# A decode kernel bound by its loads: TensorE's program in eleven rounds, another split of wo, and fifteen small unused transfers on SyncE's queue

## The chip, the cores and the metric

The kernel runs on one core of a Trainium2 chip. The metric is device time in microseconds (us) of one execution, the median of several; lower is better. Three runs of the kernel before took 675.99, 676.03 and 676.4 us. A profile is one further execution, recorded by the hardware; its span goes from the first to the last recorded instruction.

## The reference

One decode step for two sequences (B = 2, D = 448): a cached attention with 16 heads of 256, 4096 keys and values each, a small dense block with ReLU, and a gate that mixes the two.

```python
g = sigmoid((x * gate_w).sum(-1, keepdims=True))
q = (x @ wq).reshape(B, 1, H, Dh)                      # H = 16, Dh = 256
p = softmax(einsum("bhqd,bhkd->bhqk", q, k_cache) * Dh ** -0.5)
a = einsum("bhqk,bhkd->bhqd", p, v_cache).reshape(B, 1, H * Dh) @ wo
b = maximum(x @ w1, 0) @ w2                            # w1: 448 x 1792, w2: 1792 x 448
return g * a + (1 - g) * b
```

All arrays are float32. The caches alone are 2 x 134 MB.

## The kernel before, in words

The work is cut into U = 32 units, one per head and sequence. A unit is one array `kv[u]` of 128 rows of 16384 numbers (8.4 MB): 8192 of keys, 8192 of values. SBUF holds three units, `slot[0]` to `slot[2]`, and everything that is loaded goes through these slots.

**SyncE (SP)** issues every transfer, in program order, on one queue. At the start it issues `wq` into slot 0 (together with x and the gate's weights) and units 0 and 1 into slots 1 and 2. Then, unit by unit, it waits until VectorE has freed a slot (`freed`) and issues the load of the unit three further on (L166, L169). The last unit comes in two halves, keys (L171) and values (L172). Behind it, as slots come free, SP issues `w1` and `w2` of the dense block into slot 0 (L174, L175) and `wo` into slot 1 (L179). `wo` is 32 chunks of 448 columns, 0.23 MB each, and goes out in parts: the parts of `ACC`, of 14 and 9 chunks, then those of `DIRECT`, of 4, 2, 2 and 1. Each part has its own semaphore. Last, SP waits for the result (`res_ok`) and stores it (L182).

**TensorE (PE)** first does the gate (L196) and the two halves of the projection of q (L207), whose contraction of 448 is three chunks of 128 rows and one of 64. A written matmul call of float32 stands in the trace as two LDWEIGHTS and two MATMUL. Each unit's scores are 16 calls (L121, in `unit_pe`). Ten rounds of a loop do three units each, and the last two units stand behind the loop, written out. Then comes the tail: the hidden layer (L234, in `hidden`), small transposes and sums for the softmax over the four groups of keys (L241, L245, L251), the hidden layer's transposes (L256, L258), its second product (L264) and `wo`. The chunks of `ACC` are added to `acc`, on top of the second product, one call of 448 columns a chunk (L276), four column groups in turn. VectorE copies `acc` to `a_sb` (L368), four calls fold it into `z` (L284), and the chunks of `DIRECT` go straight into `z`, four calls of 112 columns a chunk (L289).

**VectorE (DVE)** takes for each unit the maximum of the scores (L135) and, after ScalarE's exponentials (L128), eight multiply-and-sum passes over the values (L141); the last one raises `freed`. It also spreads x into `xr` at the start (L336) and copies `z` to `res` at the end (L370).

The order of all this is written by hand: each engine's instructions run in the order of the text and wait on semaphores.

Of the kernel before, what the change touches and what calls it, by code (L numbers as in the profile page):

```python
# [19 lines left out]
def gated_mix_decode(nc, wq, kv, wm, wo, out):  # L20
    U, _, SW = kv.shape
    D = 448
    B = 2
    RB = R // B
    T, DH = 2, 256
# [18 lines left out]
    def ev():  # L44
        sems.append(nc.alloc_semaphore(f"e{len(sems)}"))
        return sems[-1]
# [13 lines left out]

    out_sem = nc.alloc_semaphore("out_sem")
    slot_in = [ev() for _ in range(SLOTS)]
    last_v, w1_in, w2_in = ev(), ev(), ev()
    wo_in = [ev() for _ in ACC + DIRECT]
    scored, maxed, raised, queried, freed = (ev() for _ in range(5))

# [5 lines left out]
    sel = sb("sel", P, R)  # L72
    par = sb("par", P, B)
    fold = sb("fold", P, RB, B)
    xr = sb("xr", P, KC, P // B, B)
    ge = sb("ge", P, 1)
    gp = sb("gp", P, 1)
    omg = sb("omg", P, 1)
# [6 lines left out]
    p = sb("p", P, SG)  # L85
# [10 lines left out]
    pa = ps("pa", P, CW)  # L96
# [2 lines left out]
    acc = ps("acc", P, CW)  # L99
    z = ps("z", P, CW)  # L100

    def rows_of(c, i=0):
        return slice(0, P) if c < KF else slice(i * HP, (i + 1) * HP)

    def x_of(r, c, n=R):
        return xr[r, c].rearrange("p r b -> p (r b)")[:, :n]

    xg = slot[0][:, NW:wq.shape[1]].rearrange("p (c b) -> p c b", c=KC)

    ident_0, ident_ok, par_ok = ev(), ev(), ev()  # L110
# [34 lines left out]
    LOOP = (U - 2) // SLOTS  # L145
    U1 = LOOP * SLOTS
# [8 lines left out]
    with nc.Block(no_gpsimd_drain=True) as block:  # L155

        @block.sync
        def _(_e):
            sp.wait_ge(q_mm, 2)
            sp.dma_start(slot[0], kv[2]).then_inc(slot_in[0], 16)  # L160
            with nc.Fori(0, LOOP - 1, engines=(ET.SP,)) as r:
# [12 lines left out]
            sp.dma_start(w1, wm[:, :W1]).then_inc(w1_in, 16)  # L174
            sp.dma_start(w2, wm[:, W1:]).then_inc(w2_in, 16)  # L175
            sp.wait_ge(freed, U - 1)
            k = 0
            for n, s in zip(ACC + DIRECT, wo_in):
                sp.dma_start(w_o[:, k * D:(k + n) * D], wo[:, k * D:(k + n) * D]).then_inc(s, 16)  # L179
                k += n  # L180
            sp.wait_ge(res_ok, 1)
            sp.dma_start(out, res[0:7 * 15 + 1:7, :]).then_inc(out_sem, 16)  # L182

        @block.gpsimd
        def _(_e):
            pool.memset(ident, 0.0).then_inc(ident_0, 1)
            pool.wait_ge(ident_0, 1)
# [3 lines left out]
        @block.tensor  # L191
        def _(_e):
            pe.wait_ge(x_ok, 1)
            for c in range(KC):
                r = rows_of(c)
                m = pe.matmul(pa[:, :1], x_of(r, c, P), xg[r, c, B:], start=(c == 0), stop=(c == KC - 1))  # L196
            m.then_inc(gate_mm, 1)
            W = 2 * KF * DH
            for i in range(2):
                w = slot[0][:, i * NW // 2:(i + 1) * NW // 2]  # L200
                if i:
                    pe.wait_ge(q_ok, i)
                for c in range(KC):
                    for g in range(G):
                        r = rows_of(c, g // 2)
                        at = g * W + c * CW if c < KF else G * W + g % 2 * CW
                        m = pe.matmul(pb[g * R:(g + 1) * R, :], x_of(r, c), w[r, at:at + CW], start=(c == 0),  # L207
                                      stop=(c == KC - 1))
                m.then_inc(q_mm, 1)
                pe.wait_ge(q_ok, i + 1)  # L210
                if i:
                    pe.wait_ge(qt_ok, i)
                else:
                    pe.wait_ge(ident_ok, 1)
                for k in range(2 * T):
                    m = pe.transpose(pc[:, k * P:(k + 1) * P], q[:, k * P:(k + 1) * P], ident)
                m.then_inc(q_tr, 1)
            with nc.Fori(0, LOOP, 1, engines=(ET.PE,)) as r:
                for k in range(SLOTS):
                    s = (k + 1) % SLOTS  # L220
                    unit_pe(k, r * SLOTS + (k + 1), r * 16 + (32 if s == 0 else 16), s)
            for k in range(U - U1):
                s = (k + 1) % SLOTS
                unit_pe(k, U1 + k + 1, LOOP * 16 + 16, s)

            half = W1 // 2

            def hidden(lo, hi):
                for c in range(lo, hi):
                    for g in range(G):  # L230
                        j, i = divmod(g, 2)
                        at = i * half + (j * KF + c if c < KF else 2 * KF) * FG
                        r = rows_of(c, j)
                        m = pe.matmul(pa[g * R:(g + 1) * R, :FG], x_of(r, c), w1[r, at:at + FG], start=(c == 0),  # L234
                                      stop=(c == KC - 1))
                return m
# [6 lines left out]
            hidden(2, 3)  # L243
# [3 lines left out]
            hidden(3, 4).then_inc(hid_mm, 1)  # L247
            pe.wait_ge(os_ok, 1)
            n = HH * B * J
            for g in range(G):  # L250
# [27 lines left out]
                    k += 1  # L278
            m.then_inc(acc_mm, 1)
            for i, a in enumerate(DIRECT):  # L280
                if i == FOLD_AT:
                    pe.wait_ge(a_ok, 1)
                    for g in range(G):
                        pe.matmul(z[g * R:(g + 1) * R, :DG], fold.rearrange("p r b -> p (r b)"),  # L284
                                  a_sb[:, g * DG:(g + 1) * DG], start=(i == 0), stop=False)
                pe.wait_ge(wo_in[len(ACC) + i], 16)
                for _ in range(a):
                    for g in range(G):
                        m = pe.matmul(z[g * R:(g + 1) * R, :DG], o_of(k),  # L289
                                      w_o[:, k * D + g * DG:k * D + (g + 1) * DG], start=(k == n and FOLD_AT > 0),  # L290
                                      stop=(k == NO - 1))
                    k += 1
            m.then_inc(z_mm, 1)

        @block.scalar
        def _(_e):
# [11 lines left out]
            with nc.Fori(0, LOOP, engines=(ET.Activation,)) as r:  # L308
# [20 lines left out]
        def _(_e):  # L329
# [6 lines left out]
            dve.tensor_copy(xr, xg[:, :, None, :B].to_broadcast([P, KC, P // B, B])).then_inc(x_ok, 1)  # L336
# [6 lines left out]
            with nc.Fori(0, LOOP, engines=(ET.DVE,)) as r:  # L343
# [87 lines left out]
```

## Time and profile before

| what | value |
|---|---|
| median of three runs | 676.03 us |
| the profiled execution's own time | 675.96 us |
| its span | 674.4 us |
| busy, share of the span | PE 32%, DVE 50%, ACT 7% |
| loaded | 289.5 MB, 429 GB/s over the span |
| instructions recorded | 3971 |

The shares of busy time are means over the whole span. Loads run through the whole of it, in the order in which SP issued them, and a transfer is spread over 16 DMA engines. A row of the timeline reads: start, duration, engine, line, operation, tiles, count, and in brackets how long the engine was idle before it and what ended that. In a row of the stretches (windows), the last two columns are the mean busy share of the 16 DMA engines and the GB/s moved.

### The profile page before, as it was taken

To read this page: it belongs to the slowest core of one execution; us is meant where nothing else is said; L and a number is where in the kernel's file an instruction comes from. 1 tells how busy PE (TensorE), PEld (TensorE's weight loads), DVE (VectorE), ACT (ScalarE), POOL (GpSimd) and SP (SyncE) were. 2 spreads that over 40 slices of the span, in tenths; PEclk is the share of its full clock that TensorE was granted. 3 is DMA by queue.
4 is the path that set the end of the run, shared out by engine and by line. 5 is a ranking of instruction groups with operands and counts; after the bars stand their busy time and mean duration, and the time that the engine had idled before them with its cause. 6 is when DMAs were issued, how large, how long until landed. Compare 5 with 4: busy or idle time off the path is not lost.

```text
span 674.4 us, 3971 instructions
## 1 busy us (share of the span) xinstructions
PE 218.0 (32%) x1309; PEld 53.4 (8%) x1309; DVE 340.4 (50%) x563; ACT 46.3 (7%) x107; POOL 0.7 (0%) x6
## 2 busy tenths in 40 slices
PE   0733221333332123333322233333222333332445
PEld 0200000000000000000000000000000000000012
DVE  0024566545455665544656654455666445456760
ACT  0010000000000000000000000000000000000110
POOL 0000000000000000000000000000000000000000
PEclk9975667767655666766666676665567667655869
DMA  9999999999999999999999999999999999999997
GB/s 381 428 436 435 436 435 435 435 435 435 435 435 435 435 435 435 435 435 435 431 435 435 435 435 435 435 435 435 435 431 435 435 435 435 435 435 408 423 439 303
DMA packets 6084, 289.61 MB, mean 429 GB/s; under 512 B 704, under 2 KB 832, under 8 KB 1216
## 3 DMA queue, kind: packets, MB, share of 16 engines
q1 hardware_dynamic: 6080, 289.55, 99.3%
q8 instruction: 3, 0.05, 0.0%
q14 instruction: 1, 0.01, 0.0%
HBM read 289.54 MB, written 0.01 MB: 429 GB/s over the span
## 4 chain that ended last, share of the span: by engine, by line
DMA 70%; DVE 13%; PE 10%; issue 6%; ACT 1%; DVEq 1%; SPq 0%; ACTq 0%
DMA slot<-in_kv 65%; DVE slot L141 11%; PE sc L121 9%; DMA slot<-in_wo 4%; DVE nm L135 2%; ACT p L128 1%; DVEq L141 1%; PE acc L276 0%; PE z L289 0%; SPq L166 0%; DVE a_sb L368 0%; DVEq L135 0%; ACTq L128 0%; PE z L284 0%; SPq L67 0%
## 5 line engine op out<-in xcount | busy, mean ns | idle before, releaser
L121 PE MATMUL sc<-slot,qc 128*32 128x512 f32 x1024 | 187.2, 898 | 413.1 <-DMA slot<-in_kv 413.1
L141 DVE SCALAR_TENSOR_TENSOR slot<-slot,p 128x1024 f32<-128x1024 f32 x256 | 295.9, 1222 | 47.2 <-ACT p L128 45.8
L135 DVE TENSOR_REDUCE nm<-sc 128x1024 f32 (+1 forms) x32 | 39.2, 1225 | 243.4 <-PE sc L121 243.4
L121 PEld LDWEIGHTS sc<-slot,qc 128*32 128x32 f32 x1024 | 42.0, 156 | 557.6 <-issue 538.6
L128 ACT ACTIVATE p<-sc,nm 128x1024 f32<-128x1024 f32 x32 | 35.6, 1113 | 563.2 <-DVE nm L135 563.2
L141 DVE DVE_READ_ACCUMULATOR slot<-slot,p (+1 forms) x256 | 21.3, 83 | 0.0
L207 PE MATMUL pb<-slot,xr 128*32 128x512 f32 (+1 forms) x64 | 9.5, 732 | 0.0
L336 DVE COPY xr<-slot 128x512 f32<-128x512 f32 x1 | 0.4, 426 | 17.9 <-DMA slot<-in_wq 17.9
L234 PE MATMUL pa<-slot,xr 128*32 128x448 f32 (+1 forms) x32 | 5.2, 761 | 12.3 <-DMA slot<-in_wm 12.3
L196 PE MATMUL pa<-slot,xr 128*128 128x1 f32 (+1 forms) x8 | 2.0, 357 | 20.7 <-DVE xr L336 20.7
L368 DVE COPY a_sb<-acc 128x448 f32<-128x448 f32 x1 | 0.6, 625 | 14.0 <-PE acc L276 14.0
L276 PE MATMUL acc<-slot,oc 128*32 128x448 f32 x46 | 5.6, 542 | 4.2 <-DMA slot<-in_wo 4.2
L128 ACT ACTIVATION_READ_ACCUMULATOR p<-sc,nm (+1 forms) x32 | 6.2, 193 | 0.0
L130 ACT ACTIVATE qc<-qt 128x2 f32 (+1 forms) x31 | 5.9, 192 | 0.0
L264 PE MATMUL acc<-slot,hr 128*32 128x448 f32 x28 | 3.2, 541 | 1.0 <-ACT hr L323 1.0
L196 PEld LDWEIGHTS pa<-slot,xr 128*128 128x128 f32 (+1 forms) x8 | 1.9, 322 | 20.7 <-DVE xr L336 20.7
L207 PEld LDWEIGHTS pb<-slot,xr 128*32 128x32 f32 (+1 forms) x64 | 2.0, 129 | 5.9 <-issue 5.9
L276 PEld LDWEIGHTS acc<-slot,oc 128*32 128x32 f32 x46 | 1.7, 109 | 8.1 <-issue 5.8
L234 PEld LDWEIGHTS pa<-slot,xr 128*32 128x32 f32 (+1 forms) x32 | 0.9, 140 | 14.8 <-DMA slot<-in_wm 13.2
L289 PE MATMUL z<-slot,oc 128*32 128x112 f32 x72 | 1.9, 259 | 0.0
L301 ACT ACTIVATE q<-pb 128x512 f32<-128x512 f32 x2 | 1.2, 597 | 9.1 <-PE pb L207 9.1
L364 DVE COPY oc<-pc 128x256 f32<-128x256 f32 x4 | 1.4, 418 | 0.7 <-PE pc L251 0.7
(45 smaller groups left out, 16.9 us busy)
## 6 DMA issues: line engine op xcount, KB each, us to landing
slot<-in_kv SPq DMA_DIRECT2D x2, 4096.0 KB, 34.9
slot<-in_wq SPq DMA_DIRECT2D x1, 7174.0 KB, 19.4
slot<-in_wm SPq DMA_DIRECT2D x2, 3136.0 KB, 31.2
slot<-in_wo SPq DMA_DIRECT2D x1, 3136.0 KB, 24.6
slot<-in_wo SPq DMA_DIRECT2D x1, 2016.0 KB, 29.0
slot<-in_wo SPq DMA_DIRECT2D x1, 896.0 KB, 30.7
slot<-in_wo SPq DMA_DIRECT2D x2, 448.0 KB, 31.6
slot<-in_kv SPq DMA_DIRECT2D x31, 39.7
```

The lines of the kernel that those rows point to most:

```text
L121: m = pe.matmul(sc[g * R:(g + 1) * R, c * CW:(c + 1) * CW], qc[:, s, t:t + 1].to_broadcast([P, R]), slot[s][:, lo:lo + CW], start=(t == 0) ...
L128: act.activation(p, sc, AF.Exp, bias=nm[:, bass.ds(u, 1)], accum_out=ls[:, bass.ds(u, 1)]).then_inc(raised, 1)
L130: act.activation(qc[:, s_next, :], qt[:, bass.ds(u + 1, 1), :].rearrange("p o t -> p (o t)"), AF.Copy).then_inc(queried, 1)
L135: dve.tensor_reduce(nm[:, bass.ds(u, 1)], sc, axis=AX.X, op=ALU.max, negate=True).then_inc(maxed, 1)
L141: m = dve.scalar_tensor_tensor(v, v, 1.0, p, op0=ALU.mult, op1=ALU.mult, accum_out=ov[:, bass.ds(u, 1), j].rearrange("p o -> p o"))
L196: m = pe.matmul(pa[:, :1], x_of(r, c, P), xg[r, c, B:], start=(c == 0), stop=(c == KC - 1))
L207: m = pe.matmul(pb[g * R:(g + 1) * R, :], x_of(r, c), w[r, at:at + CW], start=(c == 0), stop=(c == KC - 1))
L234: m = pe.matmul(pa[g * R:(g + 1) * R, :FG], x_of(r, c), w1[r, at:at + FG], start=(c == 0), stop=(c == KC - 1))
L264: pe.matmul(acc[g * R:(g + 1) * R, :D], hr[:, k, :], w2[:, k * D:(k + 1) * D], start=(k < G), stop=False)
L276: m = pe.matmul(acc[g * R:(g + 1) * R, :D], o_of(k), w_o[:, k * D:(k + 1) * D], start=False, stop=(k >= n - G))
L289: m = pe.matmul(z[g * R:(g + 1) * R, :DG], o_of(k), w_o[:, k * D + g * DG:k * D + (g + 1) * DG], start=(k == n and FOLD_AT > 0), stop=(k = ...
L364: m = dve.tensor_copy(oc[:, h], pc[:, h * B * J:(h + 1) * B * J].rearrange("p (o b j) -> p j o b", o=1, b=B) .to_broadcast([P, J, RB, B]))
```

## The change

It has four parts.

1. **TensorE's program gets shorter.** All 32 units run in one loop of eleven rounds. A round does units 0 and 1 of three, then asks whether it is the last, and does the third unit only if not. The other engines' loops keep their ten rounds and the two units behind them.
2. **The last 64 rows of the contraction are done for two groups at once.** A new tile `xl` (128 x 64, cleared by GpSimd, filled by two copies of VectorE) holds x for both halves of the rows, with zeros elsewhere, so that two calls of 128 rows and 64 columns take the place of four calls of 64 rows and 32 columns. `xn` holds x for the gate's last chunk. A function `project` does this for the projection of q and for the hidden layer; the arrays are laid out on the host to match.
3. **`wo` goes out in other parts**: 14, 8 and 4 chunks into `acc`, then 3, 2 and 1 straight into `z`. There are six transfers, as before.
4. **Fifteen small transfers** stand behind `wo` on SP's queue. SP waits until all 32 units are freed, then reads n rows of 256 + 16 n columns of `wo`, for n from 15 down to 1, into slot 2, which nobody reads any more. At its end, behind the store of the result, SP waits until they have landed.

```diff
-ACC = (14, 9)
-DIRECT = (4, 2, 2, 1)
-FOLD_AT = 0
+ACC = (14, 8, 4)
+DIRECT = (3, 2, 1)
...
+    def project(dst, w, at, at_last, n, lo, hi):
+        for c in range(lo, min(hi, KF)):
+            for g in range(G):
+                m = pe.matmul(dst[g * R:(g + 1) * R, :n], x_of(c), w[:, at(c, g):at(c, g) + n], start=(c == 0), stop=False)
+        if hi == KC:
+            for i in range(2):
+                m = pe.matmul(dst[i * HP:(i + 1) * HP, :n], xl.rearrange("p j r b -> p (j r b)"),
+                              w[:, at_last(i):at_last(i) + n], start=False, stop=True)
+        return m
...
             for n, s in zip(ACC + DIRECT, wo_in):
                 sp.dma_start(w_o[:, k * D:(k + n) * D], wo[:, k * D:(k + n) * D]).then_inc(s, 16)
                 k += n
+            sp.wait_ge(freed, U)
+            for n in range(15, 0, -1):
+                w = 256 + 16 * n
+                sp.dma_start(slot[2][:n, n * CW:n * CW + w], wo[:n, :w]).then_inc(small_in, 16)
             sp.wait_ge(res_ok, 1)
             sp.dma_start(out, res[0:7 * 15 + 1:7, :]).then_inc(out_sem, 16)
+            sp.wait_ge(small_in, 16 * 15)
...
-            with nc.Fori(0, LOOP, 1, engines=(ET.PE,)) as r:
-                for k in range(SLOTS):
-                    s = (k + 1) % SLOTS
-                    unit_pe(k, r * SLOTS + (k + 1), r * 16 + (32 if s == 0 else 16), s)
-            for k in range(U - U1):
-                s = (k + 1) % SLOTS
-                unit_pe(k, U1 + k + 1, LOOP * 16 + 16, s)
+            with nc.Fori(0, LOOP, engines=(ET.PE,)) as r:
+                u0 = pe.snap(r * SLOTS)
+                def units(lo, hi):
+                    for k in range(lo, hi):
+                        unit_pe(k, u0 + (k + 1), r * 16 + (32 if k == SLOTS - 1 else 16), (k + 1) % SLOTS)
+                units(0, FULL)
+                with pe.If_lt(pe.to_reg(r), LOOP - 1):
+                    units(FULL, SLOTS)
+                pe.end_ifs()
...
             dve.wait_ge(slot_in[0], 16)
-            dve.tensor_copy(xr, xg[:, :, None, :B].to_broadcast([P, KC, P // B, B])).then_inc(x_ok, 1)
+            dve.tensor_copy(xr, xg[:, :KF, None, :B].to_broadcast([P, KF, P // B, B]))
+            dve.tensor_copy(xn, xg[:, KF:, :B].to_broadcast([P, P // B, B]))
+            dve.wait_ge(xl_0, 1)
+            for j in range(2):
+                m = dve.tensor_copy(xl[j * HP:(j + 1) * HP, j], xg[j * HP:(j + 1) * HP, KF:, :B]
+                                    .to_broadcast([HP, RB, B]))
+            m.then_inc(x_ok, 1)
```

The built programs show what moves. On TensorE, from the loop of the units to the hidden layer, the rows before are these (`sc` are the scores, `qc` the unit's q, `pa` the hidden layer):

```order
L121 MATMUL sc<-slot_50,qc 32x512 x16
L116 REGISTER_ALU
L121 MATMUL sc<-slot_51,qc 32x512 x16
L115 REGISTER_ALU
L116 REGISTER_ALU
L121 MATMUL sc<-slot_49,qc 32x512 x16
L218 REGISTER_ALU
L218 COMPARE_AND_BRANCH
L121 MATMUL sc<-slot_50,qc 32x512 x16
L121 MATMUL sc<-slot_51,qc 32x512 x16
L234 MATMUL pa<-slot_49,xr 32x448 x8
```

At the same place of the changed program stand these:

```order
L129 MATMUL sc<-slot_50,qc 32x512 x16
L124 REGISTER_ALU
L129 MATMUL sc<-slot_51,qc 32x512 x16
L236 COMPARE_AND_BRANCH
L123 REGISTER_ALU
L124 REGISTER_ALU
L129 MATMUL sc<-slot_49,qc 32x512 x16
L236 UNCONDITIONAL_BRANCH
L228 REGISTER_ALU
L228 COMPARE_AND_BRANCH
L109 MATMUL pa<-slot_49,xr 32x448 x8
```

The two written-out units behind the loop are gone, 32 calls, and a branch stands ahead of the third unit. With the other parts, TensorE's program goes from 229 written matmul calls to 182.

On SP, from `wo` on, the rows before are these:

```order
L179 DMA slot_50<-in_wo 128x6272
L179 DMA slot_50<-in_wo 128x4032
L179 DMA slot_50<-in_wo 128x1792
L179 DMA slot_50<-in_wo 128x896 x2
L179 DMA slot_50<-in_wo 128x448
L182 DMA out<-res 16x112
```

In the changed program `wo` (L189) is cut otherwise, and the small transfers (L194), of which the first six are shown, stand between it and the store:

```order
L189 DMA slot_50<-in_wo 128x6272
L189 DMA slot_50<-in_wo 128x3584
L189 DMA slot_50<-in_wo 128x1792
L189 DMA slot_50<-in_wo 128x1344
L189 DMA slot_50<-in_wo 128x896
L189 DMA slot_50<-in_wo 128x448
L194 DMA slot_51<-in_wo 15x496
L194 DMA slot_51<-in_wo 14x480
L194 DMA slot_51<-in_wo 13x464
L194 DMA slot_51<-in_wo 12x448
L194 DMA slot_51<-in_wo 11x432
L194 DMA slot_51<-in_wo 10x416
```

The store of the result is now sixteenth behind the last part of `wo` on this queue instead of first.

More of the change, by code (lines that the diff above doesn't have):

```diff
@@ L62, in gated_mix_decode @@
     slot_in = [ev() for _ in range(SLOTS)]
-    last_v, w1_in, w2_in = ev(), ev(), ev()
+    last_v, w1_in, w2_in, small_in = (ev() for _ in range(4))
     wo_in = [ev() for _ in ACC + DIRECT]
@@ L100, in gated_mix_decode, with x_of @@
     z = ps("z", P, CW)
[L102 to L106, printed above, removed]
+    def x_of(c, n=R):
+        return xr[:, c].rearrange("p r b -> p (r b)")[:, :n]
+    def project(dst, w, at, at_last, n, lo, hi):
[7 more added lines that the diff above has]
+        return m
     xg = slot[0][:, NW:wq.shape[1]].rearrange("p (c b) -> p c b", c=KC)
-    ident_0, ident_ok, par_ok = ev(), ev(), ev()
+    ident_0, ident_ok, par_ok, xl_0 = ev(), ev(), ev(), ev()
     x_ok, gate_mm, gate_ok, ge_ok, gp_ok, omg_ok = (ev() for _ in range(6))
@@ L160, in _ @@
             sp.dma_start(slot[0], kv[2]).then_inc(slot_in[0], 16)
-            with nc.Fori(0, LOOP - 1, engines=(ET.SP,)) as r:
+            with nc.Fori(0, LOOP - 2, engines=(ET.SP,)) as r:
                 u0 = sp.snap(r * SLOTS)
@@ L189, in _, with pe_main @@
                                channel_multiplier=1).then_inc(ident_ok, 1)
-        @block.tensor
-        def _(_e):
+        def pe_main():
             pe.wait_ge(x_ok, 1)
             for c in range(KC):
-                r = rows_of(c)
-                m = pe.matmul(pa[:, :1], x_of(r, c, P), xg[r, c, B:], start=(c == 0), stop=(c == KC - 1))
+                r = slice(0, P if c < KF else HP)
+                m = pe.matmul(pa[:, :1], x_of(c, P) if c < KF else xn[r].rearrange("p r b -> p (r b)"), xg[r, c, B:],
+                              start=(c == 0), stop=(c == KC - 1))
             m.then_inc(gate_mm, 1)
@@ L199, in _ @@
             for i in range(2):
-                w = slot[0][:, i * NW // 2:(i + 1) * NW // 2]
                 if i:
                     pe.wait_ge(q_ok, i)
[L203 to L209, printed above, removed]
+                project(pb, slot[0][:, i * NW // 2:(i + 1) * NW // 2], lambda c, g: g * W + c * CW,
+                        lambda i: G * W + i * CW, CW, 0, KC).then_inc(q_mm, 1)
                 pe.wait_ge(q_ok, i + 1)
@@ L217, in _, with pe_tail @@
                 m.then_inc(q_tr, 1)
-            with nc.Fori(0, LOOP, 1, engines=(ET.PE,)) as r:
-                for k in range(SLOTS):
-                    s = (k + 1) % SLOTS
-                    unit_pe(k, r * SLOTS + (k + 1), r * 16 + (32 if s == 0 else 16), s)
-            for k in range(U - U1):
-                s = (k + 1) % SLOTS
-                unit_pe(k, U1 + k + 1, LOOP * 16 + 16, s)
+            with nc.Fori(0, LOOP, engines=(ET.PE,)) as r:
[7 more added lines that the diff above has]
+                pe.end_ifs()
+        def pe_tail():
             half = W1 // 2
             def hidden(lo, hi):
[L229 to L236, printed above, removed]
+                return project(pa, w1, lambda c, g: g // 2 * half + (g % 2 * KF + c) * FG,
+                               lambda i: i * half + 2 * KF * FG, FG, lo, hi)
             pe.wait_ge(w1_in, 16)
@@ L242, in _ @@
             pe.transpose(pc[:U, P:2 * P], ls, ident).then_inc(ml_tr, 1)
-            hidden(2, 3)
+            hidden(2, KF)
             pe.wait_ge(wb_ok, 1)
@@ L246, in _ @@
                       stop=True).then_inc(wp_mm, 1)
-            hidden(3, 4).then_inc(hid_mm, 1)
+            hidden(KF, KC).then_inc(hid_mm, 1)
             pe.wait_ge(os_ok, 1)
@@ L289, in _ @@
                         m = pe.matmul(z[g * R:(g + 1) * R, :DG], o_of(k),
-                                      w_o[:, k * D + g * DG:k * D + (g + 1) * DG], start=(k == n and FOLD_AT > 0),
+                                      w_o[:, k * D + g * DG:k * D + (g + 1) * DG], start=False,
                                       stop=(k == NO - 1))
@@ L293, in _ @@
             m.then_inc(z_mm, 1)
+        @block.tensor
+        def _(_e):
+            pe_main()
+            pe_tail()
         @block.scalar
@@ L307, in _ @@
             act.activation(qc[:, 1, :], qt[:, 0, :], AF.Copy).then_inc(queried, 1)
-            with nc.Fori(0, LOOP, engines=(ET.Activation,)) as r:
+            with nc.Fori(0, LOOP - 1, engines=(ET.Activation,)) as r:
                 u0 = act.snap(r * SLOTS)
@@ L342, in _ @@
             dve.tensor_scalar(omg, gp, -1.0, 1.0, op0=ALU.mult, op1=ALU.add).then_inc(omg_ok, 1)
-            with nc.Fori(0, LOOP, engines=(ET.DVE,)) as r:
+            with nc.Fori(0, LOOP - 1, engines=(ET.DVE,)) as r:
                 u0 = dve.snap(r * SLOTS)
@@ L405 @@
     full = full.reshape(P, KF, 2, G, 2 * DH).transpose(2, 0, 3, 1, 4).reshape(2, P, -1)
-    last = last.reshape(HP, 2, 2, 2, 2 * DH).transpose(1, 2, 0, 3, 4).reshape(2, P, -1)
+    last = last.reshape(HP, 2, 2, 2, 2 * DH).transpose(1, 3, 0, 2, 4).reshape(2, P, -1)
     wq = np.concatenate([full, last], 2)
@@ L410 @@
     full, last = blocks(B_w1)
-    full = full.reshape(P, KF, 2, 2, FG).transpose(0, 3, 2, 1, 4).reshape(P, 2, -1)
-    last = last.reshape(HP, 2, 2, FG).transpose(1, 0, 2, 3).reshape(P, 2, FG)
+    full = full.reshape(P, KF, 2, 2, FG).transpose(0, 2, 3, 1, 4).reshape(P, 2, -1)
+    last = last.reshape(HP, 2, 2, FG).transpose(2, 0, 1, 3).reshape(P, 2, FG)
     w1 = np.concatenate([full, last], 2).reshape(P, -1)
```

12 lines of the change are left out of this document (8 added, 4 removed).

## The prediction

> **What bounds the kernel now.** I read the chain that ended last first, then the GB/s by slice, then the end of the chain in order of time, and last the stretches of the final microseconds. From the page:
>
> ```profile
> GB/s 381 428 436 435 436 435 435 435 435 435 435 435 435 435 435 435 435 435 435 431 435 435 435 435 435 435 435 435 435 431 435 435 435 435 435 435 408 423 439 303
> ...
> DMA 70%; DVE 13%; PE 10%; issue 6%; ACT 1%; DVEq 1%; SPq 0%; ACTq 0%
> ...
> L121 PE MATMUL sc<-slot,qc 128*32 128x512 f32 x1024 | 187.2, 898 | 413.1 <-DMA slot<-in_kv 413.1
> ```
>
> The loads move 435 GB/s in nearly every slice, so no engine holds them up for long. TensorE's scores are busy for 187.2 us and idle for 413.1 us before them, every time until a load: 12.9 us a unit (413.1 / 32). What a microsecond of engine work is worth is decided only behind the last load. The chain there, from the window 600 to 676 us (start, us, what):
>
> ```profile
> 637.47 0.33 SPq L179
> ...
> 637.84 29.02 DMA slot<-in_wo
> ...
> 666.90 2.46 PE acc L276 x18
> ...
> 669.38 0.64 DVE a_sb L368
> ...
> 670.06 0.40 PE z L284 x8
> ...
> 670.46 1.77 PE z L289 x72
> ...
> 672.25 0.28 DVE res L370
> ```
>
> `wo` is issued at 637.5 and the chain then runs through the second part's landing, `acc`, `a_sb`, the fold and `z`. The transfers of that window, with KB each and us from issue to landing, and the six issues by themselves:
>
> ```profile
> slot<-in_wm SPq DMA_DIRECT2D x1, 3136.0 KB, 34.7
> slot<-in_wo SPq DMA_DIRECT2D x1, 3136.0 KB, 24.6
> slot<-in_wo SPq DMA_DIRECT2D x1, 2016.0 KB, 29.0
> slot<-in_wo SPq DMA_DIRECT2D x1, 896.0 KB, 30.7
> slot<-in_wo SPq DMA_DIRECT2D x2, 448.0 KB, 31.6
> slot<-in_wo SPq DMA_DIRECT2D x1, 224.0 KB, 32.0
> out<-res SPq DMA_DIRECT2D x1, 7.0 KB, 1.7
> ```
>
> ```profile
> L179 SPq DMA_DIRECT2D slot<-in_wo x6: 328/432/433, 637.5 to 639.7; - x6
> ```
>
> The last part is issued at 639.7 and lands 32.0 later, at 671.7. `z` is ready at 672.2, the store is issued at 672.55 and lands 1.7 later, at 674.3; the span ends at 674.4. So from the last landing to the end there are 2.7 us, and before it a queue of loads that never runs dry.
>
> **The start and the loop: no cost.** VectorE makes four copies where it made one, and TensorE four calls of 128 rows where it made eight of 64 (L207, two halves of the projection). The rows are from the timeline, then from the groups with shapes apart:
>
> ```profile
> 20.21 0.43 DVE L336 COPY xr<-slot 128x512 f32<-128x512 f32 x1 [17.94 <-DMA slot<-in_wq]
> ...
> 39.64 5.61 PE L121 MATMUL sc<-slot,qc 128*32 128x512 f32 x32 [4.87 <-DMA slot<-in_kv]
> ...
> 647.34 3.21 PE L234 MATMUL pa<-slot,xr 128*32 128x448 f32 x16 [12.26 <-DMA slot<-in_wm]
> ```
>
> ```profile
> L207 PE MATMUL pb<-slot,xr 64*32 64x512 f32 x16 | 2.1, 601 | 0.0
> ...
> L234 PE MATMUL pa<-slot,xr 64*32 64x448 f32 x8 | 1.0, 548 | 0.0
> ```
>
> The trace has no such copies and calls, so bounds: the copies add between 0 and 1.3 us (three more at 0.43), the calls change their 2.1 us by between -1.05 (half as many) and +1.05. At the worst q is 2.35 us late. TensorE waits 4.87 us for unit 0 at that place, and the next load that q releases is queued behind unit 1, so the cover holds and the term is 0. Without cover it would be up to 2.35 us. The branch in each of eleven rounds lies in 12.9 us of idle time a unit: 0. The hidden layer's last calls (1.0 us, changed by at most half of it either way) lie ahead of a wait for `wo` of 2.69 us (the row comes below): 0.
>
> [...]
>
> **The split of wo.** The rows that carry it are from the timeline, and the spread of L289's starts from that line's own view:
>
> ```profile
> 662.23 3.20 PE L276 MATMUL acc<-slot,oc 128*32 128x448 f32 x28 [2.69 <-DMA slot<-in_wo]
> ...
> 666.90 2.44 PE L276 MATMUL acc<-slot,oc 128*32 128x448 f32 x18 [1.47 <-DMA slot<-in_wo]
> ...
> 670.27 1.91 PE L289 MATMUL z<-slot,oc 128*32 128x112 f32 x72
> ```
>
> ```profile
> L289 PE MATMUL z<-slot,oc x72: 259/259/260, 670.3 to 671.9; 128*32 128x112 f32 x72
> ```
>
> From 662.2 to 666.9 nine chunks land, 0.52 us each; from there to 671.7 nine more, 0.53 each. The bytes and their order stay, so in the changed kernel the parts land at 662.2, 666.4 (eight chunks), 668.5 (four), 670.1 (three), 671.2 (two) and 671.7 (one). `acc`: a chunk is two recorded matmuls; 28 took 3.20 and 18 took 2.44, so the eight chunks take 1.8 to 2.2 and are through at 668.2 to 668.6. The four chunks' eight matmuls take between 0.9 (8 x 3.20 / 28) and 1.3 (two such steps of 0.37, and a last matmul's length of 0.54), so `acc` ends at 669.4 to 669.9; it was 669.34. The copy and the fold follow as before, so the first chunk of `z` starts at 670.3 to 670.8, where it was 670.27. Their pace is 0.023 us a matmul ((671.9 - 670.3) / 71). Ahead of the last chunk stand 40 matmuls (five chunks of eight): 0.92 us, and TensorE comes to the last chunk at 671.3 to 671.7. Before it was 64 of them, 1.47 us, and 671.74. The last chunk itself lands at 671.7 in both. From there 8 x 0.023 and the last one's 0.26 give 672.15, against 672.18 now. **So this part is worth between -0.05 and +0.1 us; I take 0.** Twelve calls fewer buy nothing, because they stood ahead of a landing.
>
> **The small transfers.** They can cost SP's time, the queue's time, or the store's. The rows are from the timeline, and the last one from SP's waits:
>
> ```profile
> 637.47 2.70 SPq L179 DMA_DIRECT2D slot<-in_wo  x6
> ...
> 649.16 0.08 DVE L141 DVE_READ_ACCUMULATOR slot<-slot,p 128x1 f32 x1
> ...
> 672.55 0.59 SPq L182 DMA_DIRECT2D out<-res  x1
> ```
>
> ```profile
> SPq L182 <- DVE res L370: 32.4, 1, 32.4
> ```
>
> SP's time: the last unit is freed at 649.2. Fifteen issues at 0.43 are 6.5 us, so SP is through at 655.7 and waits for the result from there; it waits 32.4 us now, and 16.8 us of that remain. 0. The queue's time: the small ones stand behind `wo` and are issued after it, so they can't delay it. Their bytes are 4 x the sum of n (256 + 16 n), 0.20 MB: 0.46 us at 435 GB/s if all engines share them. How they are shared no row shows; the worst is that the fifteen first rows, 23 KB, run on one engine at a sixteenth of 435 GB/s: 0.85 us. They begin at 671.7 at the latest and are through by 672.2 to 672.6. The store's first bytes come after its issue's end at 673.14 (until 673 nothing moves, by the stretches below). So 0, with a bound of +0.9 if they run late. [...] The wait at SP's end is met before the store lands: 0.
>
> **TensorE's shorter program and the end of the loads.** The stretches of the last microseconds (PE, PEld, DVE, ACT, POOL busy, clock, DMA share, GB/s), then the queues on the page and in the stretch 665 to 667 us:
>
> ```profile
> 669.00:670.00 1.00, 0.34 (x1) 0.00 (x0) 0.62 (x1) 0.00 (x0) 0.00 (x0) 1.00 0.85 333
> 670.00:671.00 1.00, 0.94 (x40) 0.94 (x44) 0.01 (x1) 0.00 (x0) 0.00 (x0) 1.00 0.23 90
> 671.00:672.00 1.00, 1.00 (x52) 0.94 (x40) 0.00 (x0) 0.00 (x0) 0.00 (x0) 1.00 0.05 18
> 672.00:673.00 1.00, 0.18 (x8) 0.00 (x0) 0.28 (x1) 0.00 (x0) 0.00 (x0) 1.00 0.00 0
> ```
>
> ```profile
> q8 instruction: 3, 0.05, 0.0%
> ```
>
> ```profile
> q8 instruction: 1, 0.02, 3.0%
> ```
>
> From 670 to 671 a quarter of the 16 engines is at work, and then less: about four engines finish late, and the last of them sets 671.7. Shared evenly, 0.85 + 0.23 + 0.05 engine-us would be done at 670.1, about 1.3 us before the last bytes. Three 16 KB transfers of queue q8, instructions, run in the span, one each in the stretches 43 to 45, 633 to 635 and 665 to 667; each takes one engine for 0.96 us (3.0% of 16 engines in 2 us), and those engines' loads come later. A program of 182 calls instead of 229 could lose one of them. But the wait is for the latest engine, and if one of several equally late ones goes, nothing moves: between 0 and -1.3 us, and I take 0, which is nearest to a row with about four late engines.
>
> [...]
>
> **Sum.** 0 for each part: the profiled execution's 675.96 stays, 1.56 above its span; the median of the runs shown is 0.07 above it. **I predict 676.0 us.**
>
> **Rivals.**
>
> *A full queue, slower.* SP's queue may hold few transfers. In the trace nine are under way at 639.7 (the last values, w1, w2, six of `wo`) and no issue is longer for it: 0.43. If nine were all, two small ones would get in at 649.2 (w2 and `wo` make seven), and one more at each landing, w2 (654.7) and the six parts; six would be left at 671.7, 2.6 us of issues, and the store would start at 674.3, not 672.55: +1.8, 677.8. It decides from fewer than thirteen places on. For it: the trace never shows more than nine. Against: none of the nine was slowed. 0.13.
>
> *Fewer instruction transfers, faster.* If the engine with the instruction transfer of 665 to 667 was alone the latest and that transfer goes, or the late engines go together, the last landing comes 0.3 to 1.3 us earlier and all behind it too, since the `acc` chain moves with the landings: 675.7 to 674.7. For it: the stretches above. Against: 0.23 of 16 engines at work means nearly four late ones, and no row says that one of them is later than the rest by more than 0.3. 0.17, of which 0.09 lie below 674.7.
>
> *The store is late.* Small transfers, or an instruction transfer (0.96 us) that now comes later, run on an engine as the store's rows come: +0.3 to +0.9, 676.3 to 676.9. 0.12.
>
> *The change doesn't take.* If the shorter program still needs three instruction transfers ahead of the last landing, it is the forecast's time again; it has no chance of its own.
>
> **How the numbers follow.** The forecast has 0.58: 676.0, from 675.8 to 676.3 by the bounds above. The range of 675.2 to 676.9 takes in the late store and half of the faster rival; out of it are the full queue (0.13) and the far half of the faster one. A measurement of this kernel tells about 0.2% (1.35 us) from no change. Faster by more needs the whole of the late engines: 0.09. Slower by more needs the full queue, or several late terms at once (0.03): 0.16. Within: 0.75.
>
> **What would show it.** In the changed profile: SP's wait ahead of the store near 17 us, and the fifteen issues at 0.43 from 649 on (a full queue shows as long issues, or a store issued later than 672.6). The last part of `wo` landing at 671.7 and the first matmul of its chunk right after; `acc` ending by 669.9. The q8 rows: how many, and when. The DMA share from 670 to 672: if it still tails off over four engines, the forecast's step holds; if it drops at once, the faster rival's. The store's landing at 1.7. The forecast is wrong if the unit loads no longer move 435 GB/s, which nothing above provides for.

## The result: 0.25% slower, and the profile after

The changed kernel took a median of 677.99 us (677.36 to 678.48, 12 runs), the kernel before, beside it on the same chip, 676.2 us (675.83 to 676.47, 12 runs). The ratio is 1.0025, 95% interval 1.0017 to 1.0033: slower by 1.8 us, a small loss whose interval lies clear of 1, where no change was forecast. The profiled execution took 677.37 us with a span of 675.7 (before 675.96 and 674.4), so it belongs to the fastest of its runs and shows 1.4 us of the 1.8. A second part comes in with the experiments.

On the page the rate of the loads is what it was until the last slices, which tells that the loss lies at the end:

```profile
GB/s 381 427 435 435 435 435 435 435 435 435 435 435 435 435 435 435 435 435 435 435 435 435 435 435 435 435 435 435 435 435 435 435 435 435 435 435 431 429 429 285
```

The chain, from 640 us on, runs through a landing of `wo` to the end, but through a later part than before:

```profile
639.05 33.54 DMA slot<-in_wo
...
672.64 0.95 PE z L297 x24
...
673.61 0.27 DVE res L389
```

The timeline says which parts are late:

```profile
666.53 1.71 PE L284 MATMUL acc<-slot,oc 128*32 128x448 f32 x16 [0.96 <-DMA slot<-in_wo]
668.67 0.96 PE L284 MATMUL acc<-slot,oc 128*32 128x448 f32 x8 [0.43 <-DMA slot<-in_wo]
669.70 0.62 DVE L387 COPY a_sb<-acc 128x448 f32<-128x448 f32 x1 [14.63 <-PE acc L284]
670.59 0.76 PE L297 MATMUL z<-slot,oc 128*32 128x112 f32 x24
672.64 0.90 PE L297 MATMUL z<-slot,oc 128*32 128x112 f32 x24 [1.29 <-DMA slot<-in_wo]
673.91 0.60 SPq L196 DMA_DIRECT2D out<-res  x1
```

Up to the first three chunks of `z` (670.59) everything comes where the prediction put it. Then TensorE waits 1.29 us for the part of two chunks. In the DMA view the parts of two and of one were under way 33.5 and 33.6 us, against 32.0 for the last one before, and landed at 672.6 and near 673.1, where 671.2 and 671.7 were forecast:

```profile
slot<-in_wo SPq DMA_DIRECT2D x1, 448.0 KB, 33.5
slot<-in_wo SPq DMA_DIRECT2D x1, 224.0 KB, 33.6
...
out<-res SPq DMA_DIRECT2D x1, 7.0 KB, 1.8
```

The stretches of the last microseconds show what the DMA engines did instead (the last two columns are their mean busy share and GB/s):

```profile
670.00:671.00 1.00, 0.62 (x28) 0.62 (x32) 0.32 (x1) 0.00 (x0) 0.00 (x0) 1.00 0.74 162
671.00:672.00 1.00, 0.35 (x16) 0.11 (x6) 0.00 (x0) 0.00 (x0) 0.00 (x0) 1.00 0.34 48
672.00:673.00 1.00, 0.36 (x16) 0.35 (x16) 0.00 (x0) 0.00 (x0) 0.00 (x0) 1.00 0.13 38
```

The two columns have to be read together. Before, a share of 0.23 moved 90 GB/s from 670 to 671, or 391 GB/s if all engines were at work. Now 0.74 move 162 (219 for all), and in the next row 0.34 move 48 (141 for all). That isn't the size of the rows alone. With the same rows written to every ninth partition (a kernel of the experiments below), the stretch from 670 to 671 moves 192 GB/s at a share of 0.57, or 337 for all:

```profile
670.00:671.00 1.00, 0.75 (x32) 0.73 (x32) 0.20 (x1) 0.00 (x0) 0.00 (x0) 1.00 0.57 192
```

So the engines that are busy here move little. From 670 to 671, 0.77 of the engines stood idle before, and 0.26 do now; the records of single rows (below) show small rows there, from 669.75 on, and rows of `wo` beside them until 672.08.

SyncE's issues did get slow, and it cost nothing. First SyncE's view of L194 (ns, minimum, median, maximum), then its wait ahead of the store:

```profile
L194 SPq DMA_DIRECT2D slot<-in_wo x15: 287/368/1812, 648.9 to 659.8; - x15
```

```profile
SPq L196 <- DVE res L389: 13.0, 1, 13.0
```

The fifteen took 12.0 us (648.92 to 660.9) and not 6.5. But SyncE was through at 660.9 and still waited 13.0 us for `res`.

### The profile page after: what moved, and what is told of

The parts are those of the page before. It is cut to its first block, busy times and chain, and to the rows that moved or that the text cites. A ratio compares the mean times of both kernels' runs of the same rounds, so it can differ in the third digit from the quotient of the medians.

```text
span 675.7 us, 3945 instructions
## 1 busy us (share of the span) xinstructions
PE 213.2 (32%) x1279; PEld 52.1 (8%) x1279; DVE 340.9 (50%) x566; ACT 46.4 (7%) x107; POOL 0.8 (0%) x7
## 4 chain that ended last, share of the span: by engine, by line
DMA 70%; DVE 13%; PE 9%; issue 6%; ACT 1%; DVEq 1%; SPq 0%; ACTq 0%
DMA slot<-in_kv 65%; DVE slot L149 11%; PE sc L129 9%; DMA slot<-in_wo 5%; DVE nm L143 2%; ACT p L136 1%; DVEq L149 1%; SPq L189 0%; PE z L297 0%; SPq L176 0%; DVEq L143 0%; ACTq L136 0%; SPq L66 0%; ACTq L135 0%; DVE res L389 0%
## 5 line engine op out<-in xcount | busy, mean ns | idle before, releaser
L129 PE MATMUL sc<-slot,qc 128*32 128x512 f32 x1024 | 183.1, 880 | 417.4 <-DMA slot<-in_kv 417.4
L211 PE MATMUL pa<-slot,xr 128*128 128x1 f32 x6 | 1.4, 356 | 21.3 <-DVE xl L353 21.3
L109 PE MATMUL pa<-slot,xr 128*32 128x448 f32 x24 | 4.2, 820 | 11.7 <-DMA slot<-in_wm 11.7
L109 PE MATMUL pb<-slot,xr 128*32 128x512 f32 x48 | 6.9, 720 | 0.0
L211 PEld LDWEIGHTS pa<-slot,xr 128*128 128x128 f32 x6 | 1.4, 327 | 21.3 <-DVE xl L353 21.3
L112 PE MATMUL pb<-slot,xl 128*64 128x512 f32 x8 | 2.2, 618 | 0.0
L109 PEld LDWEIGHTS pb<-slot,xr 128*32 128x32 f32 x48 | 1.6, 132 | 3.7 <-issue 3.7
```

The lines of the kernel that those rows point to most:

```text
L109: m = pe.matmul(dst[g * R:(g + 1) * R, :n], x_of(c), w[:, at(c, g):at(c, g) + n], start=(c == 0), stop=False)
L112: m = pe.matmul(dst[i * HP:(i + 1) * HP, :n], xl.rearrange("p j r b -> p (j r b)"), w[:, at_last(i):at_last(i) + n], start=False, stop=True)
L129: m = pe.matmul(sc[g * R:(g + 1) * R, c * CW:(c + 1) * CW], qc[:, s, t:t + 1].to_broadcast([P, R]), slot[s][:, lo:lo + CW], start=(t == 0) ...
L211: m = pe.matmul(pa[:, :1], x_of(c, P) if c < KF else xn[r].rearrange("p r b -> p (r b)"), xg[r, c, B:], start=(c == 0), stop=(c == KC - 1))
```

## The experiments

Three theories stood against each other. **Beside wo:** the small transfers delay the last rows of `wo`, for one of several reasons: their destination (rows crowded into few partitions), their source, their bytes or their number. **Not the small transfers:** the loop, the calls of 64 columns or the split lose the time. **The instruction transfers:** TensorE's shorter program moves its 16 KB instruction transfers, and one meets the store or the late rows. Where an expectation names a theory by a letter, A1 is the crowded destination, A5 its broad form (it slows every engine that is late) and C the instruction transfers. All medians but that of the change (12) are of 11 runs (the last two kernels: 5), the ratios against the kernel before on the same chip, with 95% intervals.

### Without the small transfers, and the small transfers alone

The first leaves out the wait for `freed`, the fifteen transfers and the wait at SyncE's end. The second is the kernel before with only those added.

```diff
-            sp.wait_ge(freed, U)
-            for n in range(15, 0, -1):
-                w = 256 + 16 * n
-                sp.dma_start(slot[2][:n, n * CW:n * CW + w], wo[:n, :w]).then_inc(small_in, 16)
...
-            sp.wait_ge(small_in, 16 * 15)
```

> The changed kernel without the fifteen small transfers (and without SP's two waits for them); loop, split of wo and the 64-column calls stay. Theory A (the small transfers slow the last two parts of wo on the engines that are still late): the last part lands near 671.7 us, as before, the DMA share from 671 to 672 falls back to about 0.05, and the time is 676.0 to 676.3, ratio 0.999 to 1.001 to before. Rival B (the loop, the split or TensorE's later instruction transfer cost the time): it stays at 677.5 or more, ratio 1.002 or more.

> The kernel before with the fifteen small transfers alone added. Theory A: slower by 1.2 to 2.0 us, ratio 1.0018 to 1.003, with the last parts of wo landing 1 to 1.5 us later than 671.7. Rival B: within 0.4 us of before, ratio up to 1.0006.

Without them the time is that of the kernel before: 676.13 us, 1.0001 [0.9992, 1.0010]. With them alone it is 677.49, 1.0019 [1.0010, 1.0028]. The end of `z`, first without them, then with them alone:

```profile
670.34 1.72 PE L292 MATMUL z<-slot,oc 128*32 128x112 f32 x48
```

```profile
670.52 1.33 PE L294 MATMUL z<-slot,oc 128*32 128x112 f32 x48
673.02 0.91 PE L294 MATMUL z<-slot,oc 128*32 128x112 f32 x24 [1.17 <-DMA slot<-in_wo]
```

Without them no wait is left inside `z`; with them alone the old split waits 1.17 us as the new one does 1.29. So the second theory falls, and the small transfers cause the wait.

### Where they write: every eighth, every ninth partition, partitions 64 to 78

```diff
-                sp.dma_start(slot[2][:n, n * CW:n * CW + w], wo[:n, :w]).then_inc(small_in, 16)
+                sp.dma_start(slot[2][0:8 * n:8, n * CW:n * CW + w], wo[:n, :w]).then_inc(small_in, 16)
```

Every ninth is `slot[2][0:9 * (n - 1) + 1:9, ...]`, and partitions 64 to 78 are `slot[2][HP:HP + n, ...]`. Number, bytes and source stay.

> The changed kernel with the small transfers written to every eighth partition (0, 8, 16, ...) instead of partitions 0 to 14; same bytes, same source, same counts. Theory A1 (what is shared is the way into a few neighbouring partitions): most of the loss goes, 676.0 to 676.8. Rival A2 (what is shared is the source, fifteen rows of wo read again and again, or the mere number of small packets): no change, 677.4 to 678.5.

> The changed kernel with the small transfers written to every ninth partition (0, 9, 18, ... 126); same bytes, same source, same counts. Every eighth partition moved the end of z from 673.5 back to 672.9 in the profile. [...] Rival A4 (the spread helps only through the addresses' distance): as with every eighth, z ends at 672.8 to 673.0.

> The changed kernel with the small transfers written to partitions 64 to 78 instead of 0 to 14; all else the same. Theory A1: the late engines are hurt only if their own rows go in by the same ways, so if all of them write partitions below 64 the loss of the last landing goes (z ends near 672.2), and if not all, some of it stays. Rival A5 (any fifteen neighbouring partitions hurt every late engine, as by a queue that all engines share): z ends near 673.5 as in the change.

| destination | median (range), us | ratio [95%] | wait inside `z`, us |
|---|---|---|---|
| partitions 0 to 14 (the change) | 677.99 (677.36 to 678.48) | 1.0025 [1.0017, 1.0033] | 1.29 |
| partitions 64 to 78 | 677.99 (677.42 to 678.53) | 1.0026 [1.0017, 1.0035] | 1.44 |
| every eighth | 677.29 (676.28 to 678.40) | 1.0015 [1.0006, 1.0024] | 0.44 |
| every ninth | 676.66 (676.22 to 678.23) | 1.0010 [1.0001, 1.0019] | 0.17 |

The waits are from these rows of the second group of `z`: partitions 64 to 78, every eighth, every ninth.

```profile
672.82 1.25 PE L297 MATMUL z<-slot,oc 128*32 128x112 f32 x24 [1.44 <-DMA slot<-in_wo]
```

```profile
671.98 0.88 PE L297 MATMUL z<-slot,oc 128*32 128x112 f32 x24 [0.44 <-DMA slot<-in_wo]
```

```profile
671.40 0.97 PE L297 MATMUL z<-slot,oc 128*32 128x112 f32 x24 [0.17 <-DMA slot<-in_wo]
```

The same rows in other places cost 1.4, 0.4 and 0.2 us of waiting: the destination decides. Each wait is of one profiled execution. By its median every ninth partition stands out, while every eighth, expected at 676.0 to 676.8, missed that and can't be told from the change. That any small row beside the late ones is dear falls with the every-ninth kernel. A narrower form, that a late engine suffers only if its own partitions lie near the crowded ones, gets no support from partitions 64 to 78, which cost as much as 0 to 14. It isn't excluded, since late engines may lie near both places and no row names an engine.

The trace's records of single rows show the slowing itself. Without the small transfers every row of the part of two chunks (3584 bytes) takes 140 ns. In the changed kernel the small rows run from 669.75 to 672.87, and beside them seven of those rows take 298 to 462 ns. With partitions 64 to 78 the longest takes 464 ns, with every ninth partition 194. What sets the order of the waits (1.29 and 1.44, 0.44, 0.17 us) no run here shows.

### What they carry: another source, rows of 64 bytes

```diff
-                sp.dma_start(slot[2][:n, n * CW:n * CW + w], wo[:n, :w]).then_inc(small_in, 16)
+                sp.dma_start(slot[2][:n, n * CW:n * CW + w], kv[0][:n, :w]).then_inc(small_in, 16)
```

The other kernel keeps the source and sets `w = 16`, 7.7 KB in all.

> The changed kernel with the small transfers read from the first rows of a unit of kv instead of wo; same bytes, same partitions. Theory A1 (destination): no change, 677.4 to 678.5. Rival A2 (source: the same rows of wo): the loss shrinks, 676.0 to 677.0. If it is the number of small packets alone, neither this nor the spread partitions change anything.

> The changed kernel with each row of a small transfer cut to 16 columns (64 bytes), so 120 rows and fifteen transfers as in the change but 7.7 KB instead of 202 KB. Theory A1 (bytes that crowd into a few partitions): the loss of the last landing goes, z ends near 672.2, 676.1 to 676.8. Rival A3 (the number of small packets and of their counts slows the late engines): z still ends near 673.5, 677.3 or more.

Another source changes little: 677.5 us, 1.0022 [1.0013, 1.0031]. Its second group of `z` starts at 672.56, where the change has 672.64:

```profile
672.56 0.89 PE L297 MATMUL z<-slot,oc 128*32 128x112 f32 x24 [0.24 <-DMA slot<-in_wo]
```

The wait is short only because TensorE came late itself: its granted clock was 0.50 from 662 to 668 in this execution, and `acc` ended at 670.63. Small rows take about 1.1 us of the 1.8 away, with the same number of transfers and packets: 676.91 (676.1 to 676.8 had been expected), 1.0009 [1.0000, 1.0018]. Their `z` runs without a wait inside:

```profile
670.90 1.70 PE L297 MATMUL z<-slot,oc 128*32 128x112 f32 x48
```

So most of the price is bytes into crowded partitions, and the number of packets or the place of the source is not. What makes up the 0.7 us that small rows still cost is open.

### A longer program for TensorE

Twenty-four unused calls of one column at the start of TensorE's program (206 calls instead of 182) bring a third instruction transfer, where the profile shows one, forward.

```diff
+            pe.wait_ge(ident_ok, 1)
+            for _ in range(24):
+                pe.matmul(pc[:, :1], ident, ident[:, :1], start=True, stop=True)
```

The reason to try it stood in two of the profiles above. In the every-ninth kernel `res` was copied at 672.44, early enough for 676.2 us, yet its store took 3.2 us to land, and in the every-eighth kernel 3.0, where it is 1.7 to 1.8 elsewhere. In both an instruction transfer started in the stretch from 672 to 675. Here the every-ninth kernel's rows, first its copy, then its store and queue q8 in that stretch:

```profile
672.44 0.28 DVE L389 COPY res<-z 128x112 f32<-128x112 f32 x1 [2.24 <-PE z L297]
```

```profile
out<-res SPq DMA_DIRECT2D x1, 7.0 KB, 3.2
```

```profile
q8 instruction: 1, 0.02, 2.8%
```

2.8% of 16 engines in 3 us are 1.3 us of one engine, about what the store came late. The trace's records of single rows show the meeting: fifteen of the store's sixteen rows start from 674.00 to 674.14, and the last one at 674.93, as the instruction transfer ends (674.95). The kernel without small transfers has one in that stretch too, but it was over at 673.06, ahead of the store's rows, and the store landed in 1.8.

> The changed kernel with 24 unused matmul calls of one column at TensorE's start, where it waits 20 us for wq; they only make its program longer, 206 written calls. Theory C (in the change, TensorE's third instruction transfer comes near 672 to 674 us and in some executions runs on an engine just when the store's row for it comes): with the longer program that transfer comes before 670, the upper half of the times (677.9 to 678.5) disappears, median 677.3 to 677.6. Rival: times spread from 677.4 to 678.5 as in the change, median near 678.0.

> The small transfers write every ninth partition, and TensorE gets 24 unused one-column matmuls at its start, which bring its third instruction transfer forward. If the loss has two parts, rows that crowd into a few partitions and an instruction transfer that comes as the store's rows do, both are gone: a median of 676.2 to 676.6 and runs that lie within 0.8 us of each other (with every ninth partition alone they lay 2 us apart, 676.2 to 678.2). The rival, that the late instruction transfer has no part in the time: median and spread as with every ninth partition alone, 676.7 and 2 us.

> No small transfers, and the 24 unused matmuls at TensorE's start: the rounds and the split of wo alone. If the third instruction transfer of the shorter program now and then delays the store, the runs draw together: 675.9 to 676.3, where without the unused matmuls they were 675.8 to 676.95; the median stays at that of the kernel before within 0.1%. Rival: the same spread as without them.

| kernel | median (range) without the calls, us | with them | ratio with them [95%] |
|---|---|---|---|
| the change | 677.99 (677.36 to 678.48) | 677.52 (677.18 to 677.85) | 1.0019 [1.0010, 1.0028] |
| every ninth partition | 676.66 (676.22 to 678.23) | 676.57 (676.18 to 677.06) | 1.0007 [0.9998, 1.0016] |
| no small transfers | 676.13 (675.84 to 676.95) | 675.88 (675.72 to 676.38) | 0.9996 [0.9987, 1.0005] |

With the calls the third transfer lies in the stretch 667 to 671 in all three profiles (in the changed kernel that is later than the expected 670), none lies behind it, and the store lands in 1.7 to 1.8 us:

```profile
out<-res SPq DMA_DIRECT2D x1, 7.0 KB, 1.8
```

Each time the upper end of the range comes down by more than the lower one: widths of 1.12, 2.01 and 1.11 us become 0.67, 0.88 and 0.66 (at most 0.8 had been expected for the second). For the last kernel that says little, since the kernel before, measured beside it on two chips, went from 0.93 to 0.68 as well. The other two support a second part of the loss: in some executions an instruction transfer meets the store. It isn't shown for the changed kernel itself, whose profiled execution has two instruction transfers, the later one in the stretch 655 to 662, and a store that landed in 1.8. A rival that no run tests is TensorE's clock: with partitions 64 to 78 it was 0.50 from 673 on, and the second group of `z` took 1.25 us instead of 0.90. The medians move by 0.47, 0.09 and 0.25, each less than its interval, so this part's size in the median is only known as about 0.5 us or less. The last kernel, the change without its small transfers, can't be told from the kernel before.

### The small transfers ahead of wo

The reading so far was that crowded rows hurt because early engines run them beside the late engines' last rows. Here the same transfers stand ahead of `wo` on SyncE's queue instead of behind it, into columns of slots 0 and 1 that nothing uses, in neighbouring partitions and then in every ninth.

```diff
             sp.wait_ge(freed, U - 1)
+            at = [W1 + NF * D, NO * D]
+            for n in range(15, 0, -1):
+                w = 256 + 16 * n
+                i = int(1 < n < 8)
+                sp.dma_start(slot[i][:n, at[i]:at[i] + w], wo[:n, :w]).then_inc(small_in, 16)
+                at[i] += w
             k = 0
...
```

> The same fifteen transfers with the same bytes into partitions 0 to 14, but issued ahead of wo on SyncE's queue, into columns of slots 0 and 1 that nothing uses. If the loss is that small rows, run by the engines that are early, stand in the way of the last rows of wo on the engines that are late, it needs both at once at the end: here each engine has its small rows behind it before wo's last parts, the last z group begins by 671.5 and the time is 676.3 to 676.9. Rival, a price of crowded rows wherever they stand in the queue: 677.3 or more, z as late as in the changed kernel (672.6).

> The small transfers ahead of wo as in the kernel before this one, which lost 2.5 us there (wo's first part landed 664.6 instead of 662.3), but into every ninth partition. If rows crowded into neighbouring partitions flow slowly wherever they stand, and only that costs, the stream keeps its pace: wo's first part lands at 662.5 to 663.0 (the bytes alone are 0.46 us of the even rate), and the time is 676.3 to 676.9. Rival, a price of each small row, wherever it is written: wo 2 us late again and 678 or more.

Both expectations failed, and both rivals held in the main: 678.6 us (678.47 to 678.62), 1.0035 [1.0021, 1.0049], and with every ninth partition 678.13 (677.84 to 679.41), 1.0039 [1.0026, 1.0053]. The first rows of `wo` on TensorE, in neighbouring partitions, then in every ninth:

```profile
664.74 7.25 PE L286 MATMUL acc<-slot,oc 128*32 128x448 f32 x52 [5.67 <-DMA slot<-in_wo]
```

```profile
663.92 6.12 PE L286 MATMUL acc<-slot,oc 128*32 128x448 f32 x44 [4.90 <-DMA slot<-in_wo]
```

In the changed kernel this row starts at 662.37 (3.17 us of waiting). So in these two executions the rows push the whole of `wo` back by 2.4 us, and by 1.55 when spread; their bytes at the even rate are 0.46. Where this row waits for `wo` in the other kernels' profiles, it starts from 662.06 to 662.78. The stretch 650 to 655, in which most of them run, in the same order and then in the changed kernel:

```profile
650.00:655.00 5.00, 4.03 (x35) 1.49 (x31) 2.62 (x10) 0.99 (x3) 0.00 (x0) 0.93 1.00 314
```

```profile
650.00:655.00 5.00, 3.78 (x35) 1.43 (x31) 2.75 (x12) 1.03 (x3) 0.00 (x0) 1.00 1.04 387
```

```profile
650.00:655.00 5.00, 4.11 (x35) 1.44 (x31) 2.56 (x10) 0.89 (x2) 0.00 (x0) 0.94 1.05 452
```

The DMA share is 1.00, 1.04 and 1.05, and what moves is 314, 387 and 452 GB/s. SyncE issues `wo` later in both (from 642.6 and 649.8 instead of 637.3), but with a DMA share of 0.97 to 1.05 in every stretch of 5 us from 635 to 660 that can't be the loss. So the small rows cost in both places where they stood, ahead of `wo` (678.6 and 678.13 us) as behind it (677.99 and 676.66); the price needs no tail. Spread rows have a price above their bytes too, about 1.1 us here, and what makes that up no run tells apart. That crowding costs more than spreading here too, 0.8 us, is not shown: it is about what this row differs between the other profiles, and the ratios of 1.0035 and 1.0039 can't be told apart. Only the GB/s point that way.

## Why the prediction was wrong, step by step

- **"The start and the loop: no cost"**: right. With these parts and the split, and no small transfers, the ratio is 1.0001.
- **The split of `wo`, "I take 0"**: right, and so were its times. `acc` was forecast to end at 669.4 to 669.9, and its copy starts at 669.70; `z` was to start at 670.3 to 670.8, and its chunks start at 670.59. Without the small transfers `res` is copied at 672.13, where it was 672.25 before.
- **SyncE's time, 0**: right, with a wrong size. The issues took 12.0 us instead of 6.5 and the wait left was 13.0 instead of 16.8. So something like the full queue began to show (issues up to 1.81 us), though ahead of `wo` the same fifteen took at most 0.40 each, and the six of `wo` behind them 8.46 together. SyncE was never held until the last landing: it was through at 660.9. That the time comes near that rival's 677.8 is chance: its mechanism, a store issued late by SyncE, isn't in the trace.
- **"The small ones stand behind `wo` and are issued after it, so they can't delay it"**: this step failed, and with it go the 1.4 us of the profiled execution. The order in the queue wasn't the order in time. The prediction had seen that about four engines finish late, and didn't ask what the others do then. Small rows begin at 669.75, while rows of the part of two chunks run until 672.08. Written into fifteen neighbouring partitions, they make the rest slow: rows of that part take up to 462 ns instead of 140, and it lands 1.4 us late. Crowding into few partitions is shown as the cause (partitions 0 to 14 against every ninth). On which part of the way the engines meet is not.
- **The bytes, 0.46 to 0.85 us, done by 672.6**: too small for the same reason. The small rows began 2 us earlier than the 671.7 of the sum and still ended later, at 672.87. Ahead of `wo` the crowded 0.20 MB pushed the stream back by 2.4 us, five times the 0.46 of the even rate.
- **TensorE's shorter program, "0 to -1.3, I take 0"**: no gain. The changed profile has two instruction transfers instead of three, and none in the stretch 664 to 668, yet the parts of `wo` up to the three chunks landed when forecast. In the every-ninth kernel, which has none from 662 to 673, TensorE still waits for the last part until 671.97. So nothing was gained with that transfer gone. That the engines are late for another reason is likely but not shown, as every profile has either the small rows or an instruction transfer that late. The other sign had been left to the rival of the late store. That an instruction transfer now comes later was the author's estimate: the last one starts at 659.47 in the changed profile, where it was 665.77 before, and at 673.6 in the every-ninth kernel. There and in the every-eighth kernel the rival's mechanism shows, and its price is 1.2 to 1.4 us (landing 3.0 and 3.2 instead of 1.8), not 0.3 to 0.9, in some executions only.
- **What was to show it**: the share of the DMA engines from 670 to 672 was to tell the cases apart. It was 0.74 and 0.34 against 0.23 and 0.05, a case that no rival had; only with the GB/s beside it does it read as crowding.

## What to carry to other kernels

The small transfers stood behind `wo` on the queue and weren't behind it in time: their rows ran from 669.75 us on, while the kernel still waited for rows of `wo` that ran until 672.08. So a transfer that nobody waits for can be paid for at the end of a load-bound kernel (0.20 MB cost 1.8 us here, where the even rate gives 0.46), above all if its rows crowd into few neighbouring partitions. Leave it out or spread it (every ninth partition brought 1.3 us back), and don't expect it to be cheaper further ahead (678.6 and 678.1 us there). Read a stretch's DMA share and its GB/s together (0.74 with 162 GB/s here, 0.23 with 90 before), and when a program is made shorter, look where its instruction transfers go (the last one from 665.77 to 659.47 here, and to 673.6 in the every-ninth kernel).

## What the runs showed of the hardware that was not expected

- Beside loads from HBM into fifteen neighbouring partitions, rows of another transfer that take 140 ns without them took up to 462 ns (464 with partitions 64 to 78, 194 with every ninth), and 0.74 of 16 engines moved 162 GB/s, where with every ninth partition 0.57 moved 192.
- SyncE's issues of small transfers took 0.29 us at the least and up to 1.81 behind `wo`, and 0.25 to 0.40 ahead of it (0.42 to 1.03 there with every ninth partition); what sets the difference is open.
- In two profiles an instruction transfer of 16 KB (1.3 us of one engine) met the store of 7 KB, which landed in 3.0 us (every eighth partition) and 3.2 (every ninth) instead of 1.8. In the second, one of the store's sixteen rows waited: it started at 674.93, the others by 674.14.
